# Softmax exponentials per head straight from PSUM on ScalarE, and one vector operation less per weight block, in a pooled-attention and gated-product kernel

## The chip, the cores and the metric

One core of one Trainium2 chip. The metric is device time in microseconds. The engines are named as in the profile: PE is TensorE (its matmuls; PEld are its weight loads), DVE is VectorE, ACT is ScalarE, POOL is GpSimd, SP issues the DMAs. Work on different engines meets through semaphores; each engine takes its own instructions strictly in the order of the program.

## The reference

```python
# q, k, v: 8 x 8 heads x 576 x 64, fp32; k and v are averaged over groups of 8 positions
k_p = k.reshape(B, H, 72, 8, 64).mean(axis=3)
v_p = v.reshape(B, H, 72, 8, 64).mean(axis=3)
scores = scale * np.matmul(q, k_p.transpose(0, 1, 3, 2))
scores = scores - np.max(scores, axis=-1, keepdims=True)
attn = np.exp(scores)
attn = attn / (np.sum(attn, axis=-1, keepdims=True) + 1e-09)
x = np.matmul(attn, v_p)          # put together to 4608 tokens x 512
# the weights arrive as float64: 512 x 1536, 512 x 1536, 1536 x 512
return ((x @ w_a) * (x @ w_b)) @ w_out
```

## The kernel before

**Products.** The 4608 tokens form 9 tiles of 512, and the inner width 1536 forms 12 blocks of 128, so there are 108 steps, x = 0 to 107. `ffn_in(x)` computes block f of x @ w_a into the PSUM tile `psa` and of x @ w_b into `psb`, `gated` multiplies the two (ACT copies `psa` to `h`, DVE multiplies `psb` into it at L528), and `ffn_out(x - 1)` adds the step before to four accumulators `acc`. For accuracy every fp32 operand is split into a high and a low part (`jha`, `jla` and so on), and three products high·high, low·high, high·low are summed. That makes 36 matmuls of 512 columns in a step.

**Splitting the weights.** `split_weight` does it for each step anew: ACT casts the high part (L236), POOL subtracts to get the low part (L171, through the helper `low_part`). The tiles `jh…`, `jl…` have two buffers each.

**Converting the weights.** `convert_weights` runs only in the first tile. For each of 3 matrices and 12 blocks a DMA brings the float64 words into one area per matrix, and fp32 is put together from the bits: ACT takes the magnitude of the high words (`wmag`, L212) and scales the low words (`wlow`, L213); DVE clamps and scales the magnitude (L214), masks and shifts it (L215), sets the sign bit (L219) and adds the low words (L224). After L219 the area is free and the next block's load is issued. Block f + 1 is converted during step f - 1.

**Attention.** `chunk(i)` handles 128 or 64 query rows of one batch, all heads; there are 40 chunks, four of them (`early`, the first tile) before the first step. The scores of two heads (2 · 72 = 144 columns) come from one block-diagonal key tile `kdiag`. For the first 9 chunks (`SUMMED = 9`) each pair of heads takes three matmuls of 144 columns into PSUM (L390), and DVE takes the maximum (L374) and subtracts it (L375) straight from PSUM. The later 31 chunks take one matmul of 288 columns that holds the high and the low key part side by side (L404) and one of 144 (L407); DVE adds the two halves (L410), then takes maximum and difference over all 8 heads. In both forms ACT then takes the exponential of all 576 columns at once (L424), DVE sums it (L426), adds 1e-9 and inverts (L427, L428), POOL scales (L430), and the probabilities are split, transposed on PE (`ptr`, L475), copied out by ACT (`p`, L476) and multiplied with the values (`po`). The PSUM tiles of scores, transposes and values share a ring of two buffers, tag `att` (the four early chunks use the accumulators' buffers for scores).

**Order.** The order of each engine is that in which the Python code emits instructions. `Chains` holds generators that are resumed by a clock of slots: `yield n` sleeps n slots, `yield PE` waits for a turn to put matmuls between those of a step. A step makes six slots, one for each six of its matmuls.

Of the kernel before, what the change touches and what calls it, by code (L numbers as in the profile page):

```python
# [9 lines left out]
F32 = mybir.dt.float32  # L10
F32R = mybir.dt.float32r
I32 = mybir.dt.int32
U32 = mybir.dt.uint32
AF = mybir.ActivationFunctionType
ALU = mybir.AluOpType
AX = mybir.AxisListType

B, H, S, D = 8, 8, 576, 64
POOL = 8
SP = S // POOL  # L20
P = 128
# [4 lines left out]
NF = DF // P  # L26
NK = DM // P

TINY = 2.0**-15
SCALE = 1.0 / float(D) ** 0.5  # L30


# [19 lines left out]
BLOCK, BLOCK_LATER = 256, 384  # L52

NTMP = 6

SUMMED = 9

AHEAD = 2

# [12 lines left out]
class Chains:  # L72
# [4 lines left out]
    PE = "PE"  # L77
# [4 lines left out]
    def mark(self, *what):  # L82
        self.done.add(what)

    def wait(self, *marks):
        while not all(m in self.done for m in marks if not isinstance(m[-1], int) or m[-1] >= 0):
            yield 1
# [26 lines left out]
def attn_moe_kernel(ctx: ExitStack, tc: tile.TileContext, q, k, v, vr, wa, wb, wo, out):  # L114
    nc = tc.nc
    const = ctx.enter_context(tc.tile_pool(name="const", bufs=1))
    sb = ctx.enter_context(tc.tile_pool(name="sb", bufs=2))
    ps = ctx.enter_context(tc.tile_pool(name="ps", bufs=1, space=bass.MemoryType.PSUM))
    chains = Chains()
    PE = Chains.PE  # L120
    mark, wait, done = chains.mark, chains.wait, chains.done
    PRODUCTS, SPLITS, CHUNKS, WEIGHTS, KEYS = ((x, 0) for x in range(5))

    def tmp(name, dtype=F32):
        return sb.tile([P, 512], dtype, tag="tmp", name=name, bufs=NTMP)
# [20 lines left out]
    blocks, start = [], 0  # L146
# [14 lines left out]
    while start < len(flat):  # L161
        stop = start
# [3 lines left out]
        start = stop  # L166
# [28 lines left out]
    def convert_weights(name, j, first):  # L195

        def load_words(f):
            nc.sync.dma_start(area[name], w_dram[name][:, f, :].bitcast(I32))

        load_words(0)
        yield first
        for f in range(NF):
            words = area[name].rearrange("p (c w) -> p c w", w=2)
            hi, lo = words[:, :, 1], words[:, :, 0]
            w = raw[name][:, f, :]
            wi = w.bitcast(I32)  # L210
            low, mag = tmp(f"wlow_{name}{f}", I32), tmp(f"wmag_{name}{f}")
            nc.scalar.activation(mag, hi.bitcast(F32), AF.Abs)  # L212
            nc.scalar.activation(low, lo.bitcast(U32), AF.Copy, scale=2.0**-29)  # L213
            nc.vector.tensor_scalar(out=w, in0=mag, scalar1=TINY, scalar2=2.0**-16, op0=ALU.max, op1=ALU.mult)  # L214
            nc.vector.tensor_scalar(  # L215
                out=wi, in0=wi, scalar1=0x0FFFFFFF, scalar2=3, op0=ALU.bitwise_and, op1=ALU.logical_shift_left
            )
            yield 1
            nc.vector.scalar_tensor_tensor(  # L219
                out=wi, in0=hi, scalar=-(1 << 31), in1=wi, op0=ALU.bitwise_and, op1=ALU.bitwise_or  # L220
            )
            if f + 1 < NF:
                load_words(f + 1)
            nc.vector.tensor_tensor(out=wi, in0=wi, in1=low, op=ALU.add)  # L224
            mark("weight", name, f)
            yield 2

            while f + 1 >= AHEAD and (len(begun) <= f + 1 - AHEAD or chains.now < begun[f + 1 - AHEAD] + 2 * j):
                yield 1
# [116 lines left out]
    def chunk(i):  # L346
        b, o, n = flat[i]
        t, col = divmod(b * S + o, NT)
        first = i < early
# [7 lines left out]
        qh = sb.tile([P, NK, P], F32R, tag="qh", name=f"qh_{i}")  # L357
        ql = sb.tile([P, NK, P], F32R, tag="ql", name=f"ql_{i}")
# [7 lines left out]
        kd = kdiag[b % 2]  # L366
        s = sb.tile([P, H, SP], F32, tag="s", name=f"s_{i}")
        m = sb.tile([P, H], F32, tag="m", name=f"m_{i}")
        z = sb.tile([P, H], F32, tag="z", name=f"z_{i}")
        hk = 2 * SP  # L370

        def less_max(hs, src):
            nh = hs.stop - hs.start
            nc.vector.tensor_reduce(out=m[:n, hs], in_=src, axis=AX.X, op=ALU.max)  # L374
            nc.vector.tensor_tensor(  # L375
                out=s[:n, hs], in0=src, in1=m[:n, hs].unsqueeze(2).broadcast_to([n, nh, SP]), op=ALU.subtract
            )

        if i < SUMMED:
            for g0 in range(0, NK, 2):  # L380
                yield from wait(("keys", b, g0))
                yield PE
                if first:
                    pt = ps.tile([P, 512], F32, tag="acc", name=f"psc_{i}_{g0}", bufs=4)
                else:
                    pt = ps.tile([P, 512], F32, tag="att", name=f"psc_{i}_{g0}", bufs=2)
                for j in range(2):
                    g = g0 + j
                    for x, (qq, w) in enumerate(((qh, 0), (qh, 1), (ql, 0))):
                        nc.tensor.matmul(  # L390
                            pt[:n, j * hk:(j + 1) * hk],
                            qq[:, g, :n],
                            kd[:, g, w].rearrange("p e s -> p (e s)"),
                            start=(x == 0),
                            stop=(x == 2),
                        )
                less_max(slice(2 * g0, 2 * g0 + 4), pt[:n, :2 * hk].rearrange("p (h s) -> p h s", h=4))
        else:
            for g in range(NK):
                yield from wait(("keys", b, g - g % 2))  # L400
                if g % 2 == 0:
                    yield PE
                pt = ps.tile([P, 512], F32, tag="att", name=f"psc_{i}_{g}", bufs=2)
                nc.tensor.matmul(  # L404
                    pt[:n, :2 * hk], qh[:, g, :n], kd[:, g].rearrange("p w e s -> p (w e s)"), start=True, stop=False
                )
                nc.tensor.matmul(  # L407
                    pt[:n, :hk], ql[:, g, :n], kd[:, g, 0].rearrange("p e s -> p (e s)"), start=False, stop=True
                )
                nc.vector.tensor_reduce(  # L410
                    out=s[:n, 2 * g:2 * g + 2, :].rearrange("p h s -> p (h s)"),
                    in_=pt[:n, :2 * hk].rearrange("p (w c) -> p c w", w=2),
                    axis=AX.X,
                    op=ALU.add,
                )
                if g % 2 and g < NK - 1:
                    yield 1
            yield 1
            less_max(slice(0, H), s[:n])
        mark("scores", i)  # L420


        yield 1
        nc.scalar.activation(s[:n], s[:n], AF.Exp, scale=SCALE)  # L424
        yield 1
        nc.vector.tensor_reduce(out=z[:n], in_=s[:n], axis=AX.X, op=ALU.add)  # L426
        nc.vector.tensor_scalar_add(z[:n], z[:n], 1e-9)  # L427
        nc.vector.reciprocal(z[:n], z[:n])  # L428
        yield 1
# [1 line left out]
            out=s[:n], in0=s[:n], in1=z[:n].unsqueeze(2).broadcast_to([n, H, SP]), op=ALU.mult  # L431
# [17 lines left out]
        j = block_of[i]  # L449
# [47 lines left out]
        for g0 in range(0, NK, per):  # L497
# [6 lines left out]
            for g in range(g0, g0 + per):  # L504
                if per == NK and g == NK // 2:
# [9 lines left out]
                    start=False,  # L515
                    stop=True,
# [41 lines left out]
    acc = {}  # L558
# [27 lines left out]
    with tc.manual_schedule():  # L586
        load_early()
        nc.vector.tensor_copy(ident, ident0)
        for t in kdiag + vdiag:
            nc.gpsimd.memset(t.bitcast(F32), 0.0)  # L590
        nc.vector.tensor_reduce(
            out=mask[:NR], in_=ident0[:NR, :NR].rearrange("p (a c s) -> p c a s", a=3, c=4), axis=AX.XY, op=ALU.add
        )
        chains.start(load_keys(0), KEYS)
        for i in range(early):
            chains.start(chunk(i), (CHUNKS[0], i), EARLY_GAP * i)
# [3 lines left out]
        for j, name in enumerate(("a", "b", "o")):  # L600
            chains.start(convert_weights(name, j, CONVERT_AFTER + 2 * j), WEIGHTS, WEIGHTS_START)
# [6 lines left out]
        for i in range(early, len(flat)):  # L608
            b, o, n = flat[i]
            end = TILE_SLOTS * (b * S + o + n) // NT - TILE_SLOTS  # L610
            if tile_of[i] == 1:
                end = TILE_SLOTS - (tail[-1] - i) * CHUNK_GAP
            begin_at = max(0, end - (CHUNK if tile_of[i] == 1 else CHUNK_LATER))
            chains.start(chunk(i), (CHUNKS[0], i), begin_at)
            if i + 1 < len(flat) and flat[i + 1][0] > max(b, 1):
                keys_at = max(0, begin_at - KEYS_AHEAD)
                chains.start(load_keys(b + 1), KEYS, keys_at)
                chains.start(load_values(b + 1), KEYS, keys_at + VALUES_AFTER)
# [65 lines left out]
```

## Time and profile before

| | |
|---|---|
| median of 3 runs | 1110.5 us (1110.24 to 1191.36) |
| profiled execution | 1109.42 us, its span 1107.6 us |
| granted TensorE clock, mean over the span | 0.972 |
| PE busy | 1036.8 us (94%), 4964 matmuls |
| DVE busy | 601.3 us (54%) |
| ACT busy | 523.2 us (47%) |
| POOL busy | 565.4 us (51%) |
| HBM | 49.28 MB read, 9.44 MB written |

The profiled execution and the span differ by 1.8 us that lie around the first and the last instruction. A row of a group reads: line, engine, operation, tiles written and read, shapes, count; busy us and mean ns of one; idle time of the engine just before them, and what ended it. A row of the timeline reads: start, duration, engine, line, operation, tiles, shapes, count, and in brackets the idle time before it.

### The profile page before, as it was taken

How to read it: one execution, taken by the hardware profiler on the slowest of the kernel's cores; microseconds unless marked ns; L12 is line 12 of the kernel's file. 1: busy time of each engine (PE TensorE's matmuls, PEld its weight loads, DVE VectorE, ACT ScalarE, POOL GpSimd, SP SyncE). 2: the span in 40 equal slices, each digit the busy share in tenths (PEclk: the TensorE clock that was granted, in tenths of full speed). 3: DMA queues.
4: the chain of work that ended last, by engine and by line, in shares of the span. 5: the costliest groups of instructions: out<-in, count | busy, mean ns of one | idle time of the engine just before them, and what ended most of it. 6: DMA issues, size and time to landing. Idle time of an engine off the chain costs nothing.

```text
span 1107.6 us, 13659 instructions
## 1 busy us (share of the span) xinstructions
PE 1036.8 (94%) x4964; PEld 861.5 (78%) x4964; DVE 601.3 (54%) x953; ACT 523.2 (47%) x1051; POOL 565.4 (51%) x465
## 2 busy tenths in 40 slices
PE   4378887899999999999999999999999999999998
PEld 4256765688887888888888888888888888888887
DVE  8889899963348333753367335653458343332111
ACT  3654555544445445544455445444445444443332
POOL 6234353455555555555555455554556455554442
PEclk9778888999999999999999999999999999999999
DMA  6444343220023000400021002200211020001001
GB/s 221 124 142 124 121 129 120 74 89 1 1 70 111 1 1 22 148 3 1 1 94 59 1 1 91 81 1 1 69 55 48 1 67 1 1 1 38 1 1 38
DMA packets 29875, 59.59 MB, mean 54 GB/s; under 512 B 7121, under 2 KB 7121, under 8 KB 29809
## 3 DMA queue, kind: packets, MB, share of 16 engines
q1 hardware_dynamic: 29808, 58.73, 16.7%
q8 instruction: 39, 0.64, 0.2%
q14 instruction: 28, 0.22, 0.1%
HBM read 49.28 MB, written 9.44 MB: 53 GB/s over the span
## 4 chain that ended last, share of the span: by engine, by line
PE 82%; DVE 13%; ACT 2%; DMA 1%; issue 1%; POOL 0%; SPq 0%; DVEq 0%; ACTq 0%
PE acc L571 9%; PE psa L550 8%; PE psb L550 8%; PE acc L573 8%; PE acc L572 8%; PE psa L552 8%; PE psa L551 8%; PE psb L551 8%; PE psb L552 8%; PE ptr L475 2%; PE psc L404 2%; DVE wb_raw L224 1%; DVE wa_raw L224 1%; DVE wo_raw L224 1%; DVE wb_raw L219 1%
## 5 line engine op out<-in xcount | busy, mean ns | idle before, releaser
L171 POOL TENSOR_TENSOR jlb<-wb_raw,jhb 128x512 fp32r<-128x512 f32 x108 | 142.8, 1322 | 244.6 <-ACT jhb L236 244.6
L528 DVE TENSOR_TENSOR h<-psb,h 128x512 f32<-128x512 f32 x108 | 74.5, 690 | 344.1 <-PE psb L552 334.3
L171 POOL TENSOR_TENSOR jla<-wa_raw,jha 128x512 fp32r<-128x512 f32 x108 | 143.1, 1325 | 196.4 <-ACT jha L236 170.1
L555 ACT COPY h<-psa 128x512 f32<-128x512 f32 x108 | 63.3, 587 | 241.9 <-PE psa L552 234.3
L550 PE MATMUL psb<-xh,jhb 128*128 128x512 f32 x432 | 172.9, 400 | 4.6 <-DVE h L528 4.6
L571 PE MATMUL acc<-jho,hh 128*128 128x512 f32 x432 | 175.7, 407 | 0.0
L550 PE MATMUL psa<-xh,jha 128*128 128x512 f32 x432 | 172.7, 400 | 0.0
L573 PE MATMUL acc<-jho,hl 128*128 128x512 f32 x432 | 170.2, 394 | 0.6 <-DVE hl L171 0.6
L572 PE MATMUL acc<-jlo,hh 128*128 128x512 f32 x432 | 170.0, 393 | 0.0
L552 PE MATMUL psb<-xh,jlb 128*128 128x512 f32 x432 | 170.0, 393 | 0.0
L551 PE MATMUL psb<-xl,jhb 128*128 128x512 f32 x432 | 169.9, 393 | 0.0
L552 PE MATMUL psa<-xh,jla 128*128 128x512 f32 x432 | 169.6, 392 | 0.0
L551 PE MATMUL psa<-xl,jha 128*128 128x512 f32 x432 | 169.3, 392 | 0.0
L171 POOL TENSOR_TENSOR jlo<-wo_raw,jho 128x512 fp32r<-128x512 f32 x108 | 154.3, 1428 | 5.6 <-ACT jho L236 5.6
L531 ACT CAST hh<-h 128x512 fp32r<-128x512 f32 x108 | 67.1, 621 | 84.7 <-DVE h L528 84.6
L171 DVE TENSOR_TENSOR hl<-h,hh 128x512 fp32r<-128x512 f32 x108 | 93.9, 869 | 20.7 <-ACT hh L531 20.5
L550 PEld LDWEIGHTS psb<-xh,jhb 128*128 128x128 f32 x432 | 82.2, 190 | 20.9 <-issue 4.3
L573 PEld LDWEIGHTS acc<-jho,hl 128*128 128x128 f32 x432 | 81.9, 190 | 18.9 <-DVE hl L171 1.0
L552 PEld LDWEIGHTS psb<-xh,jlb 128*128 128x128 f32 x432 | 82.2, 190 | 17.6
L552 PEld LDWEIGHTS psa<-xh,jla 128*128 128x128 f32 x432 | 81.7, 189 | 17.6
L551 PEld LDWEIGHTS psb<-xl,jhb 128*128 128x128 f32 x432 | 82.2, 190 | 15.2
L551 PEld LDWEIGHTS psa<-xl,jha 128*128 128x128 f32 x432 | 82.0, 190 | 15.2 <-DVE xl L171 0.2
(92 smaller groups left out, 1714.4 us busy)
## 6 DMA issues: line engine op xcount, KB each, us to landing
out<-y SPq DMA_DIRECT2D x36, 256.0 KB, 2.2
kraw<-in_k SPq DMA_DIRECT2D x28, 288.0 KB, 3.6
vraw<-in_v SPq DMA_DIRECT2D x28, 256.0 KB, 3.0
qraw<-in_q SPq DMA_DIRECT2D x28, 256.0 KB, 3.7
words<-in_wa SPq DMA_DIRECT2D x12, 512.0 KB, 3.5
words<-in_wb SPq DMA_DIRECT2D x12, 512.0 KB, 3.6
words<-in_wo SPq DMA_DIRECT2D x12, 512.0 KB, 3.5
vraw<-in_vr SPq DMA_DIRECT2D x14, 192.0 KB, 2.5
```

Of the source, the lines that this page charges most:

```text
L171: eng.tensor_tensor(out=lo, in0=src, in1=hi.bitcast(F32), op=ALU.subtract)
L224: nc.vector.tensor_tensor(out=wi, in0=wi, in1=low, op=ALU.add)
L404: nc.tensor.matmul(pt[:n, :2 * hk], qh[:, g, :n], kd[:, g].rearrange("p w e s -> p (w e s)"), start=True, stop=False)
L528: nc.vector.tensor_tensor(out=h, in0=pt, in1=h, op=ALU.mult)
L531: nc.scalar.copy(hh, h)
L550: nc.tensor.matmul(pt, wh[:, c], xh[:, kk], start=(kk == 0), stop=False)
L551: nc.tensor.matmul(pt, wh[:, c], xl[:, kk], start=False, stop=False)
L552: nc.tensor.matmul(pt, wl[:, c], xh[:, kk], start=False, stop=(kk == NK - 1))
L555: nc.scalar.copy(h, pt)
L571: nc.tensor.matmul(acc[c], hh[:, cs], wh, start=(f == 0), stop=False)
L572: nc.tensor.matmul(acc[c], hh[:, cs], wl, start=False, stop=False)
L573: nc.tensor.matmul(acc[c], hl[:, cs], wh, start=False, stop=(f == NF - 1))
```

## The change

Three edits.

1. In `convert_weights` the magnitude comes from ACT already scaled (by 2^-112), the vector operation at L214 goes, and the masking reads ACT's result directly. The count of ACT's instructions stays.
2. In `chunk`, all 40 chunks take the form with three matmuls of 144 columns; the form with 288 columns and its sum goes.
3. The softmax is done per group of four heads: DVE takes the maximum from PSUM and multiplies it by -scale (4 columns), and ACT then runs four exponentials, one for each head, of 72 columns each, from PSUM, with the maximum as bias and with their sums written to `z`. The subtraction, the exponential over 576 columns and the sum on DVE go. All of it is emitted in the slot of the matmuls; one `yield 1` is left before the inversion.

```diff
-            nc.scalar.activation(mag, hi.bitcast(F32), AF.Abs)
+            nc.scalar.activation(mag, hi.bitcast(F32), AF.Abs, scale=SHRINK)
             nc.scalar.activation(low, lo.bitcast(U32), AF.Copy, scale=2.0**-29)
-            nc.vector.tensor_scalar(out=w, in0=mag, scalar1=TINY, scalar2=2.0**-16, op0=ALU.max, op1=ALU.mult)
             nc.vector.tensor_scalar(
-                out=wi, in0=wi, scalar1=0x0FFFFFFF, scalar2=3, op0=ALU.bitwise_and, op1=ALU.logical_shift_left
+                out=wi, in0=mag.bitcast(I32), scalar1=0x0FFFFFFF, scalar2=3, op0=ALU.bitwise_and, op1=ALU.logical_shift_left
             )
...
-        def less_max(hs, src):
-            nh = hs.stop - hs.start
-            nc.vector.tensor_reduce(out=m[:n, hs], in_=src, axis=AX.X, op=ALU.max)
-            nc.vector.tensor_tensor(
-                out=s[:n, hs], in0=src, in1=m[:n, hs].unsqueeze(2).broadcast_to([n, nh, SP]), op=ALU.subtract
-            )
-
-        if i < SUMMED:
...
-        else:
-            for g in range(NK):
...
-                nc.tensor.matmul(
-                    pt[:n, :2 * hk], qh[:, g, :n], kd[:, g].rearrange("p w e s -> p (w e s)"), start=True, stop=False
...
-                nc.tensor.matmul(
-                    pt[:n, :hk], ql[:, g, :n], kd[:, g, 0].rearrange("p e s -> p (e s)"), start=False, stop=True
...
-            less_max(slice(0, H), s[:n])
...
+        for g0 in range(0, NK, 2):
...
+            for j in range(2):
+                g = g0 + j
+                for x, (qq, w) in enumerate(((qh, 0), (qh, 1), (ql, 0))):
+                    nc.tensor.matmul(
...
+            hs = slice(2 * g0, 2 * g0 + 4)
+            scores = pt[:n, :2 * hk].rearrange("p (h s) -> p h s", h=4)
+            nc.vector.tensor_reduce(out=m[:n, hs], in_=scores, axis=AX.X, op=ALU.max)
+            nc.vector.tensor_scalar_mul(m[:n, hs], m[:n, hs], -SCALE)
+            for j in range(4):
+                h = 2 * g0 + j
+                nc.scalar.activation(
+                    s[:n, h], scores[:, j], AF.Exp, bias=m[:n, h:h + 1], scale=SCALE, accum_out=z[:n, h:h + 1]
+                )
         mark("scores", i)
...
-        nc.scalar.activation(s[:n], s[:n], AF.Exp, scale=SCALE)
-        yield 1
-        nc.vector.tensor_reduce(out=z[:n], in_=s[:n], axis=AX.X, op=ALU.add)
         nc.vector.tensor_scalar_add(z[:n], z[:n], 1e-9)
         nc.vector.reciprocal(z[:n], z[:n])
```

ACT's order around chunk 4, the first chunk after the first step, before the change. The numbers behind names count tiles as they are made, and differ between the two programs; `s_632` here and `s_645` below are the same chunk's exponentials, `h_616` and `h_630` the product of step 1.

```order
L212 ACTIVATE wmag_b_621<-words 128x512
L213 ACTIVATE wlow_b_620<-words 128x512
L236 CAST jhb_658<-wb_raw 128x512
L236 CAST jho_661<-wo_raw 128x512
L212 ACTIVATE wmag_o_665<-words 128x512
L213 ACTIVATE wlow_o_664<-words 128x512
L531 CAST hh_655<-h_616 128x512
L424 ACTIVATE s_632<-s_632 64x576
L212 ACTIVATE wmag_a_708<-words 128x512
```

The same place now:

```order
L210 ACTIVATE wmag_b_635<-words 128x512
L211 ACTIVATE wlow_b_634<-words 128x512
L392 ACTIVATE s_645,z_647<-psc_0_653,m_646 64x72 x4
L233 CAST jhb_675<-wb_raw 128x512
L233 CAST jho_678<-wo_raw 128x512
L210 ACTIVATE wmag_o_682<-words 128x512
L211 ACTIVATE wlow_o_681<-words 128x512
L392 ACTIVATE s_645,z_647<-psc_2_686,m_646 64x72 x4
L503 CAST hh_672<-h_630 128x512
```

The exponentials now stand in two groups of four, the first one ahead of the casts and magnitudes that stood ahead of the single exponential before.

DVE's order at the same place, before:

```order
L374 TENSOR_REDUCE m_633<-psc_0_640 64x4
L375 TENSOR_TENSOR s_632<-psc_0_640,m_633 64x288
L528 TENSOR_TENSOR h_616<-psb_1_618,h_616 128x512
L214 TENSOR_SCALAR wo_raw<-wmag_o_665 128x512
L215 TENSOR_SCALAR wo_raw<-wo_raw 128x512
L374 TENSOR_REDUCE m_633<-psc_2_670 64x4
L375 TENSOR_TENSOR s_632<-psc_2_670,m_633 64x288
L219 SCALAR_TENSOR_TENSOR wo_raw<-words,wo_raw 128x512
L224 ISA wo_raw<-wo_raw,wlow_o_664 128x1024
L171 TENSOR_TENSOR hl_656<-h_616,hh_655 128x512
L426 TENSOR_REDUCE z_634<-s_632 64x8
L427 TENSOR_SCALAR z_634<-z_634 64x8
```

And now:

```order
L388 TENSOR_REDUCE m_646<-psc_0_653 64x4
L389 TENSOR_SCALAR m_646<-m_646 64x4
L500 TENSOR_TENSOR h_630<-psb_1_632,h_630 128x512
L212 TENSOR_SCALAR wo_raw<-wmag_o_682 128x512
L388 TENSOR_REDUCE m_646<-psc_2_686 64x4
L389 TENSOR_SCALAR m_646<-m_646 64x4
L399 TENSOR_SCALAR z_647<-z_647 64x8
L400 RECIPROCAL z_647<-z_647 64x8
L216 SCALAR_TENSOR_TENSOR wo_raw<-words,wo_raw 128x512
L221 ISA wo_raw<-wo_raw,wlow_o_681 128x1024
L170 TENSOR_TENSOR hl_673<-h_630,hh_672 128x512
```

The addition to `z`, which needs all eight exponentials, now stands right behind the second maximum; before there were three long operations between the second subtraction and the sum.

PE's order at the first half of a later chunk's scores, before:

```order
L404 MATMUL psc_0_4415<-kdiag_73,qh_4360 128x288
L407 MATMUL psc_0_4415<-kdiag_73,ql_4361 128x144
L404 MATMUL psc_1_4419<-kdiag_73,qh_4360 128x288
L407 MATMUL psc_1_4419<-kdiag_73,ql_4361 128x144
L550 MATMUL psa_5_4400<-xh_3242,jha_4324 128x512
```

And now:

```order
L379 MATMUL psc_0_4499<-kdiag_73,qh_4466 128x144 x2
L379 MATMUL psc_0_4499<-kdiag_73,ql_4467 128x144
L379 MATMUL psc_0_4499<-kdiag_73,qh_4466 128x144 x2
L379 MATMUL psc_0_4499<-kdiag_73,ql_4467 128x144
L522 MATMUL psa_5_4485<-xh_3262,jha_4408 128x512
```

Four matmuls with 864 columns in all became six with the same 864 columns.

More of the change, by code (lines that the diff above doesn't have):

```diff
@@ L27 @@
 NK = DM // P
-TINY = 2.0**-15
+SHRINK = 2.0**-112
 SCALE = 1.0 / float(D) ** 0.5
@@ L54 @@
 NTMP = 6
-SUMMED = 9
 AHEAD = 2
@@ L370, in chunk @@
         hk = 2 * SP
-        def less_max(hs, src):
-            nh = hs.stop - hs.start
-            nc.vector.tensor_reduce(out=m[:n, hs], in_=src, axis=AX.X, op=ALU.max)
-            nc.vector.tensor_tensor(
-                out=s[:n, hs], in0=src, in1=m[:n, hs].unsqueeze(2).broadcast_to([n, nh, SP]), op=ALU.subtract
-            )
-        if i < SUMMED:
[L380 to L384, printed above, removed]
-                else:
[L386 to L398, printed above, removed]
-            for g in range(NK):
[L400 to L404, printed above, removed]
-                    pt[:n, :2 * hk], qh[:, g, :n], kd[:, g].rearrange("p w e s -> p (w e s)"), start=True, stop=False
-                )
-                nc.tensor.matmul(
-                    pt[:n, :hk], ql[:, g, :n], kd[:, g, 0].rearrange("p e s -> p (e s)"), start=False, stop=True
[L409 to L416, printed above, removed]
-                    yield 1
-            yield 1
-            less_max(slice(0, H), s[:n])
@@ new lines, in chunk @@
+        for g0 in range(0, NK, 2):
+            yield from wait(("keys", b, g0))
+            yield PE
+            if first:
+                pt = ps.tile([P, 512], F32, tag="acc", name=f"psc_{i}_{g0}", bufs=4)
+            else:
+                pt = ps.tile([P, 512], F32, tag="att", name=f"psc_{i}_{g0}", bufs=2)
+            for j in range(2):
+                g = g0 + j
+                for x, (qq, w) in enumerate(((qh, 0), (qh, 1), (ql, 0))):
+                    nc.tensor.matmul(
+                        pt[:n, j * hk:(j + 1) * hk],
+                        qq[:, g, :n],
+                        kd[:, g, w].rearrange("p e s -> p (e s)"),
+                        start=(x == 0),
+                        stop=(x == 2),
+                    )
[7 more added lines that the diff above has]
+                    s[:n, h], scores[:, j], AF.Exp, bias=m[:n, h:h + 1], scale=SCALE, accum_out=z[:n, h:h + 1]
+                )
@@ L420, in chunk @@
         mark("scores", i)
         yield 1
-        nc.scalar.activation(s[:n], s[:n], AF.Exp, scale=SCALE)
-        yield 1
-        nc.vector.tensor_reduce(out=z[:n], in_=s[:n], axis=AX.X, op=ALU.add)
         nc.vector.tensor_scalar_add(z[:n], z[:n], 1e-9)
```

## The prediction

> **What bounds the kernel now.** I read the chain that ended last, then busy time by stretch, then the groups of instructions in the stretch where the stage changes.
>
> ```profile
> PE 82%; DVE 13%; ACT 2%; DMA 1%; issue 1%; POOL 0%; SPq 0%; DVEq 0%; ACTq 0%
> 0.00:60.00 60.00, 25.59 (x122) 23.19 (x123) 50.17 (x87) 28.71 (x62) 25.50 (x35) 0.86 0.55 178
> 60.00:207.00 147.00, 116.03 (x512) 92.78 (x511) 134.99 (x199) 81.34 (x162) 61.85 (x46) 0.85 0.39 120
> 207.00:250.00 43.00, 41.40 (x209) 34.42 (x208) 29.84 (x44) 20.82 (x41) 23.33 (x18) 1.00 0.24 79
> 250.00:1108.00 858.00, 853.80 (x4127) 711.13 (x4125) 386.34 (x626) 392.34 (x788) 454.68 (x368) 1.00 0.10 33
> ```
>
> The columns of the last four rows are length, then busy us of PE, PEld, DVE, ACT, POOL, then granted clock, DMA share, GB/s. Two regimes meet at about 207 us. From 250 on PE is busy 853.8 of 858 us at clock 1.00, and nothing but fewer or shorter matmuls helps. From 60 to 207, while ten blocks of each weight matrix are converted, DVE is busy 134.99 of 147 us (92%) and PE's clock drops to 0.85 in its gaps. The 13% of DVE in the chain lie here and in the 60 us before. So each part of the change is priced by regime: on DVE before 207, on PE after.
>
> **Part 1: the vector operation at L214 goes.** These are its groups in the 60:207 stretch, with the spread of one of them over the whole run, and two neighbours that met no other engine.
>
> ```profile
> L214 DVE TENSOR_SCALAR wb_raw<-wmag_b 128x512 f32<-128x512 f32 x10 | 6.0, 596 | 2.0 <-ACT wmag_b L212 2.0
> L214 DVE TENSOR_SCALAR wa_raw<-wmag_a 128x512 f32<-128x512 f32 x10 | 5.4, 536 | 1.5 <-ACT wmag_a L212 1.5
> L214 DVE TENSOR_SCALAR wo_raw<-wmag_o 128x512 f32<-128x512 f32 x10 | 5.1, 515 | 1.4 <-ACT wmag_o L212 1.4
> L214 DVE TENSOR_SCALAR wa_raw<-wmag_a x12: 367/420/1516, 34.9 to 194.6; 128x512 f32<-128x512 f32 x12
> 78.88 0.42 DVE L214 TENSOR_SCALAR wb_raw<-wmag_b 128x512 f32<-128x512 f32 x1
> 79.33 0.43 DVE L215 TENSOR_SCALAR wb_raw<-wb_raw 128x512 int32<-128x512 int32 x1
> ```
>
> Thirty of them cost 16.5 us as recorded, but the median is 420 ns and some reach 1516. From one start to the next it is 0.45 us (79.33 - 78.88), so 30 x 0.45 = 13.5 us; the other 3 us are stretches in which an instruction was held up. I count 13.5: a hold that L214 no longer takes falls on L215 behind it. The Trainium skill, "SBUF — State Buffer", section "Who interferes with whom", says why that is likely: a DVE operation in a two-port mode and a GpSimd operation lock each other out for a whole instruction. By that rule the removal gains 13.5 us, without it 16.5.
>
> Ahead of the first step, six more L214 stand in the chain that ends last; these four are its pieces of them, and the wait that follows.
>
> ```profile
> 34.94 0.35 DVE wa_raw L214
> 42.47 0.44 DVE wa_raw L214
> 45.94 1.29 DVE wo_raw L214
> 49.01 0.35 DVE wb_raw L214
> 50.47 3.53 DMA words<-in_wo
> ```
>
> They add up to 2.4 us, of which some 0.9 in the third are a hold (1.29 against 0.42). I take 2 us: the load of `words` for `wo` is issued that much earlier, and ACT's queue (`wmag_o`, then the copies of `ptr`, then the first step) with it. The casts, DMAs and SP's queue keep their order. Sum of part 1: -15.5 us, and nothing after 207, where no conversion runs.
>
> **Part 2: three matmuls of 144 columns in place of 288 and 144.** The first six rows are half a later chunk as it is now, up to the second matmul after it; the last six are half of chunk 8, which has the new form already.
>
> ```profile
> 410.76 0.29 PE L404 MATMUL psc<-kdiag,qh 128*128 128x288 f32 x1
> 410.89 0.23 PE L407 MATMUL psc<-kdiag,ql 128*128 128x144 f32 x1
> 410.95 0.34 PE L404 MATMUL psc<-kdiag,qh 128*128 128x288 f32 x1
> 411.13 0.23 PE L407 MATMUL psc<-kdiag,ql 128*128 128x144 f32 x1
> 411.20 0.44 PE L550 MATMUL psa<-xh,jha 128*128 128x512 f32 x1
> 411.48 0.39 PE L551 MATMUL psa<-xl,jha 128*128 128x512 f32 x1
> ...
> 183.33 0.34 PE L390 MATMUL psc<-kdiag,qh 128*128 128x144 f32 x2
> 183.51 0.28 PE L390 MATMUL psc<-kdiag,ql 128*128 128x144 f32 x1
> 183.62 0.39 PE L390 MATMUL psc<-kdiag,qh 128*128 128x144 f32 x2
> 183.84 0.27 PE L390 MATMUL psc<-kdiag,ql 128*128 128x144 f32 x1
> 183.96 0.43 PE L550 MATMUL psb<-xh,jhb 128*128 128x512 f32 x1
> 184.23 0.39 PE L551 MATMUL psb<-xl,jhb 128*128 128x512 f32 x1
> ```
>
> Half a chunk moves from 411.48 - 410.76 = 0.72 us to 184.23 - 183.33 = 0.90: the columns are equal, but six weight loads stand in place of four, and short matmuls do not cover them. That is 0.36 us for a chunk. Of the 31 chunks, 25 have 128 rows: +9.0 us. The six with 64 rows load half as many columns of weights; they cost between 0 and 0.36 us each, and I take 0. PE has no slack there, so all of it counts: **+9.0 us**, at most 11.2. This is the surest term.
>
> **Part 3: the softmax per group.** From 250 on I count it at nothing. DVE loses work, ACT gains some, and the cover is that weight parts are ready long before use:
>
> ```profile
> 401.26 1.29 POOL L171 TENSOR_TENSOR jla<-wa_raw,jha 128x512 fp32r<-128x512 f32 x1 [2.50 <-ACT jha L236]
> 409.85 0.39 PE L552 MATMUL psa<-xh,jla 128*128 128x512 f32 x1
> ```
>
> `jla`, done at 402.55, is first read at 409.85, 7.3 us later; a group of exponentials that holds ACT for 2 us is hidden. In the `att` ring the next tile after a chunk's second scores comes six slots later, so four slow readers hold nobody up.
>
> Before 207 it is otherwise. Chunks 4 to 8 fall there. What DVE saves, per chunk, and what it adds:
>
> ```profile
> L426 DVE TENSOR_REDUCE z<-s 128x8 f32<-128x576 f32 x3 | 2.2, 745 | 0.0
> L375 DVE TENSOR_TENSOR s<-psc,m 128x288 f32<-128x288 f32 x6 | 2.7, 458 | 0.4
> L427 DVE TENSOR_SCALAR z<-z 128x8 f32<-128x8 f32 x3 | 1.2, 401 | 0.1
> ```
>
> Two L375 and one L426 go: 2 x 0.46 + 0.74 = 1.66 us. Two operations on 4 columns come; the nearest is L427, 0.40 us in this stretch: 0.80. So DVE's work falls by 0.86 us, 4.3 in five chunks. But now ACT stands between DVE's own instructions, and its rows price the wait.
>
> ```profile
> 78.95 0.60 ACT L236 CAST jhb<-wb_raw 128x512 fp32r<-128x512 f32 x1
> 79.46 0.61 ACT L236 CAST jho<-wo_raw 128x512 fp32r<-128x512 f32 x1
> 79.98 0.68 ACT L212 ACTIVATE wmag_o<-words 128x512 f32<-128x512 f32 x1
> 86.34 0.68 ACT L424 ACTIVATE s<-s 64x576 f32<-64x576 f32 x1 [1.01 <-DVE s L375]
> 91.28 0.39 ACT L441 CAST rem<-s 64x64 fp32r<-64x64 f32 x2
> 28.38 0.65 ACT L267 ACTIVATE kdiag<-kp 64x144 fp32r<-64x144 f32 x2
> ```
>
> No row has an exponential of 72 columns with a bias and a sum. Two casts of 64 columns take 0.39 us together, two scalings of 144 columns 0.65; above, one instruction cannot cost more than the whole of 576 columns, 0.68. Four are thus 0.7 to 2.7 us, and I take 1.1, near the scalings. By the Trainium skill, "ScalarE: Activation LUTs", section "What ACT_TABLE_LOAD costs", a per-partition bias adds about 93 ns to an activation; an estimate from its figures is 1.1 us for four as well, without the sum; no row here has such a bias.
>
> The wait comes twice in a chunk. After the first maximum DVE soon needs a `wmag` that now stands behind the exponentials and what follows them on ACT. In chunks 4 and 7 that is 1.1 + 0.51 + 0.52 + 0.68 = 2.8 us, less 0.6 for `h` on DVE: 2.2. In chunks 5 and 8 only the copy of `h` (about 0.5) stands between: 2.3. In chunk 6 nothing does, and `hl` covers 0.6: 1.2. After the second maximum `z` needs the second group: 1.1 us and a hop, 1.2. Sum: 2 x 2.2 + 2 x 2.3 + 1.2 + 5 x 1.2 = 16.2 us. Against it stand the waits for `wmag` that DVE has now, 2.0 + 1.5 + 1.4 = 4.9 us in L214's rows; about 3.4 come after an exponential and go. That leaves +12.8 us. While DVE waits, POOL finishes operations that would have held it later; with POOL busy 61.85 of 147 us, that gives back between 0 and 0.42 x 12.8 = 5.4, and I take 2. Net of part 3: -4.3 + 12.8 - 2 = **+6.5 us**. In chunks 0 to 3 DVE saves about as much as ACT adds; I count 0, within 3 us either way.
>
> **Sum.** -15.5 + 9.0 + 6.5 = 0 on the profiled execution's own 1109.42 us, of which 1107.6 are its span; the median of the runs shown, 1110.5, is 0.1% above. Forecast: **1109 us**, no change that a measurement of this kernel tells from none, which takes about 2% (22 us).
>
> **The rivals.**
>
> *The waits hide.* If ACT's groups mostly fall into DVE's stalls, part 3 is -4.3 in place of +6.5: 1098 us; with L214's holds gone too (another 3), 1095. For it: DVE is idle 12 of 147 us already, and PE runs ahead of it, so scores are ready early. Against it: `z` stands directly behind the second maximum, and nothing is between to fill that hole.
>
> *Exponentials cost what the wide one does.* If summing makes each of the eight cost 0.68 us, each group takes 2.7 in place of 1.1, and five chunks wait twice 1.6 us longer: +16, 1125 us. It turns slower than before at the 0.275 us for one exponential that I took, since the sum is 0 there; each further tenth of a microsecond adds 4 us, and over 2% it would need 0.84. For it: fixed cost dominates small rows (240 ns for 64 columns). Against it: 144 columns take 0.33.
>
> *The conversion does not hang on DVE.* If the loads of `words` or ACT's order set the pace there, L214's removal moves nothing, and part 1 is 0: 1109 + 15.5 = 1125. For it: DMAs of 3.5 us stand in the early chain. Against it: 92% DVE busy and ACT busy 81 of 147.
>
> **How the numbers follow.** Forecast, 1103 to 1115: 0.57. Waits hidden, 1091 to 1103: 0.23. Dear exponentials, 1115 to 1130: 0.12. Conversion not on DVE, 1115 to 1128: 0.08. The range that leaves out 2 in 10 is 1095 to 1120: the low end has waits hidden and holds gone, the high end 0.5 us for one exponential (+9) and all of PE's upper bound (+2.2). Faster by over 2% (below 1088) needs more than the first rival gives: 0.06. Slower by over 2% (above 1132) needs both others together: 0.05. Between: 0.89.
>
> **What would show it.** In the profile after: 124 more matmuls; scores of 128 rows at about 0.90 us for each half chunk up to the second matmul behind; no holes on PE from 250 on; L212 (the old L215) with a larger mean hold and new waits for `wmag`; `z`'s addition waiting for ACT about 1.2 us in chunks 4 to 8; ACT's exponentials near 0.27 us from start to start; the first step starting at about 57.7 in place of 59.66; the conversions done at about 198 in place of 207. The prediction is wrong if the first 250 us shrink by over 15 us, if an exponential's start-to-start is over 0.4, or if PE waits for weight parts late in the run.

## The result, and the profile after

The changed kernel takes **1127.0 us** (median of 4 runs), the kernel before 1110.5 us beside it: a ratio of 1.0149, with a 95% interval of 1.0129 to 1.0169. That is 16.5 us slower. One of the four runs of the kernel before, at 1191.36 us, fell in a slower state of the chip and is left out of these figures. The forecast was 1109 us, and the time lies above its range, 1095 to 1120. The prediction took 2% as what a measurement of this kernel needs; the interval is 0.2% to either side, so the loss is clear. The profiled span went from 1107.6 to 1124.8 us.

First the shares of the chain that ended last, where PE had 82% and ACT 2% before:

```profile
PE 76%; DVE 13%; ACT 6%; issue 3%; DMA 1%; SPq 0%; DVEq 0%; ACTq 0%
```

Then the stages, in the columns of the prediction's table (length, busy us of PE, PEld, DVE, ACT, POOL, granted clock, DMA share, GB/s):

```profile
0.00:60.00 60.00, 24.94 (x119) 22.80 (x120) 41.94 (x77) 35.81 (x121) 26.93 (x35) 1.00 0.54 178
60.00:207.00 147.00, 118.10 (x541) 93.42 (x541) 121.21 (x171) 94.60 (x245) 65.76 (x48) 0.91 0.40 124
207.00:250.00 43.00, 42.25 (x216) 35.60 (x214) 24.20 (x35) 22.77 (x69) 22.84 (x18) 1.00 0.20 67
250.00:1125.00 875.00, 862.72 (x4218) 720.41 (x4217) 362.26 (x534) 441.61 (x1217) 458.37 (x365) 0.99 0.10 32
```

DVE did get lighter, by 13.8 us in 60:207, and ACT heavier by 13.3. The stage that was full is no longer full: from 250 on PE was idle for 4.2 of 858 us before, and now for 12.3 of 875.

A second view locates that. Take the start of each of the 108 steps (its first `psa` matmul) in both traces. The changed kernel is 5.5 us ahead at step 13 (227 us). Behind that it loses 0.37 us for each chunk of 128 rows, evenly, and has **three jumps**, each over three or four steps: 4.4 us at 340 to 376 us, 2.7 at 598 to 640, 2.9 at 858 to 891. Some 3 us more go in smaller steps, which were not traced one by one. At the first jump, PE waits for a copy of `ptr` (the third transpose takes the buffer of the `att` ring that this copy frees), and ACT's copy stands behind `hh`, which waits for DVE. These rows are PE, ACT, then DVE and POOL in order of time:

```profile
353.26 0.28 PE L447 MATMUL ptr<-ident,rem 64*96 64x64 f32 x2 [3.52 <-ACT p L448]
352.23 0.62 ACT L503 CAST hh<-h 128x512 fp32r<-128x512 f32 x1 [4.18 <-DVE h L500]
344.06 6.81 DVE L328 SCALAR_TENSOR_TENSOR vdiag<-vp,vdiag 64x256 fp32r<-64x256 f32 x2
350.79 0.68 DVE L170 TENSOR_TENSOR vrem<-vwide,vrem 32x512 fp32r<-32x512 f32 x1
351.50 0.69 DVE L500 TENSOR_TENSOR h<-psb,h 128x512 f32<-128x512 f32 x1
343.65 1.49 POOL L402 TENSOR_TENSOR s<-s,z 64x576 f32<-64x576 f32 x1 [4.40 <-DVE z L400]
345.11 1.29 POOL L170 TENSOR_TENSOR jla<-wa_raw,jha 128x512 fp32r<-128x512 f32 x1
346.49 1.36 POOL L170 TENSOR_TENSOR pr<-s,pr 64x512 fp32r<-64x512 f32 x1
347.80 0.33 POOL L170 TENSOR_TENSOR rem<-s,rem 64x64 fp32r<-64x64 f32 x1
348.08 1.28 POOL L170 TENSOR_TENSOR jlb<-wb_raw,jhb 128x512 fp32r<-128x512 f32 x1
349.33 1.25 POOL L170 TENSOR_TENSOR jlo<-wo_raw,jho 128x512 fp32r<-128x512 f32 x1
```

Two operations on `vdiag` (the low part of a new batch's values) take 6.81 us on DVE, as long as POOL's row of six operations lasts without a pause. In the kernel before the same two took 1.91 us, and POOL's scaling of `s` came only eight microseconds later:

```profile
345.44 1.91 DVE L331 SCALAR_TENSOR_TENSOR vdiag<-vp,vdiag 64x256 fp32r<-64x256 f32 x2
353.56 1.33 POOL L430 TENSOR_TENSOR s<-s,z 64x576 f32<-64x576 f32 x1
```

The schedule counts in slots (the `yield` numbers). The old softmax had three more of them between a later chunk's scores and POOL's scaling: one between the two halves of the scores, one ahead of the maximum over all heads, one behind the exponential. With them gone, POOL's row of the chunk moved on top of DVE's work for the next batch's values. That was the theory to be tried; its rival was that eight exponentials at a time hold ACT, whatever the slots.

### The profile page after: what moved, and what is told of

The parts are those of the page before. It is cut to its first block, busy times and chain, and to the rows that moved or that the text cites. A ratio compares the mean times of both kernels' runs of the same rounds, so it can differ in the third digit from the quotient of the medians.

```text
span 1124.8 us, 14426 instructions
## 1 busy us (share of the span) xinstructions
PE 1048.0 (93%) x5088; PEld 872.2 (78%) x5088; DVE 549.6 (49%) x815; ACT 594.8 (53%) x1651; POOL 573.9 (51%) x465
## 4 chain that ended last, share of the span: by engine, by line
PE 76%; DVE 13%; ACT 6%; issue 3%; DMA 1%; SPq 0%; DVEq 0%; ACTq 0%
PE psb L522 8%; PE psa L522 8%; PE psa L524 8%; PE psa L523 8%; PE psb L524 7%; PE psb L523 7%; PE acc L543 7%; PE acc L544 7%; PE acc L545 7%; PE psc L379 3%; ACT s L392 3%; DVE vdiag L328 2%; PE ptr L447 2%; DVE h L500 1%; DVE hl L170 1%
## 5 line engine op out<-in xcount | busy, mean ns | idle before, releaser
L170 POOL TENSOR_TENSOR jla<-wa_raw,jha 128x512 fp32r<-128x512 f32 x108 | 155.4, 1439 | 93.0 <-ACT jha L233 88.1
L522 PE MATMUL psb<-xh,jhb 128*128 128x512 f32 x432 | 178.4, 413 | 3.1 <-DVE h L500 3.1
L543 PE MATMUL acc<-jho,hh 128*128 128x512 f32 x432 | 171.2, 396 | 0.0
L392 ACT ACTIVATE s<-psc,m 128x72 f32<-128x72 f32 (+1 forms) x320 | 97.9, 318 | 133.8 <-DVE m L389 133.2
L170 DVE TENSOR_TENSOR hl<-h,hh 128x512 fp32r<-128x512 f32 x108 | 130.3, 1206 | 38.2 <-ACT hh L503 38.0
L402 POOL TENSOR_TENSOR s<-s,z 128x576 f32<-128x576 f32 (+1 forms) x38 | 46.3, 1218 | 198.9 <-PE psb L524 122.1
```

Source lines behind the costliest of these rows:

```text
L170: eng.tensor_tensor(out=lo, in0=src, in1=hi.bitcast(F32), op=ALU.subtract)
L392: nc.scalar.activation(s[:n, h], scores[:, j], AF.Exp, bias=m[:n, h:h + 1], scale=SCALE, accum_out=z[:n, h:h + 1])
L402: (nc.vector if first and i % 2 else nc.gpsimd).tensor_tensor(out=s[:n], in0=s[:n], in1=z[:n].unsqueeze(2).broadcast_to([n, H, SP]), op=AL ...
L522: nc.tensor.matmul(pt, wh[:, c], xh[:, kk], start=(kk == 0), stop=False)
L543: nc.tensor.matmul(acc[c], hh[:, cs], wh, start=(f == 0), stop=False)
```

## The experiments

All times are medians; each ratio is to runs of the kernel before on the same chip. Where an expectation speaks of the three later batches, the edit reaches all seven batches after the first; the jumps are at three of them.

### One part at a time

The weights' edit alone, on the kernel before:

```diff
-nc.scalar.activation(mag, hi.bitcast(F32), AF.Abs)
+nc.scalar.activation(mag, hi.bitcast(F32), AF.Abs, scale=SHRINK)
-nc.vector.tensor_scalar(out=w, in0=mag, scalar1=TINY, scalar2=2.0**-16, ...)
-nc.vector.tensor_scalar(out=wi, in0=wi, ...)
+nc.vector.tensor_scalar(out=wi, in0=mag.bitcast(I32), ...)
```

> The kernel before with the weights' edit alone (the magnitude scaled in its activation, 36 vector operations fewer). Theory: DVE sets the pace to 207 us, and part 1 is worth the 15.5 us of the prediction: about 1095 us, the first step at about 57.7 us in place of 59.7, and no change in what stands after 250 us. Rival: the conversion does not hang on DVE (the loads of words or ACT's queue set it): 1109 to 1111 us.

Measured: 1097.0 us, 0.9876 (0.9862 to 0.9891), **-13.2 us**. The rival falls: the conversion does hang on DVE. Step 13 starts 12.6 us earlier, and PE has no hole from 250 on:

```profile
250.00:1095.00 845.00, 841.11 (x4065) 700.71 (x4063) 382.96 (x619) 386.02 (x774) 446.31 (x360) 1.00 0.10 33
```

But the first step starts at 59.75 us, as before, and not at 57.7. The chain of waits says why:

```profile
49.24 4.61 DMA words<-in_wo
53.94 0.66 ACT wmag_o L213
```

The load of `words` for `wo` is issued 1.2 us earlier than before (49.24 against 50.47) and takes 1.1 us longer (4.61 against 3.53). It lands at the same time. Why it took longer is not shown.

The columns alone, with the old softmax operations:

```diff
-SUMMED = 9
+SUMMED = 40
```

> The kernel before with the three matmuls of 144 columns in all chunks (they were in chunks 0 to 8 only) and the softmax in its old operations, two slots earlier from chunk 9 on since that form has fewer of them. Theory: 0.37 us for each chunk of 128 rows, about +9 us, 1120 us, with no jump at 344, 601 and 861 us. Rival 1: the jumps come from the slots that go missing, not from the exponentials: two of the four slots are gone here, so jumps of 1 to 4 us stand at those three places as well, 1123 to 1130. Rival 2: the columns cost nothing and the +0.37 us for each chunk is the exponentials' doing: 1111 us.

Measured: 1119.4 us, 1.0079 (1.0064 to 1.0094), **+9.2 us**, with 0.37 us for each chunk of 128 rows. Two of the three missing slots are missing here too, and the largest PE gap from 250 us on is 0.5 us. So those two slots alone make no jump.

Everything but the weights' edit:

```diff
-nc.scalar.activation(mag, hi.bitcast(F32), AF.Abs, scale=SHRINK)
+nc.scalar.activation(mag, hi.bitcast(F32), AF.Abs)
+nc.vector.tensor_scalar(out=w, in0=mag, scalar1=TINY, scalar2=2.0**-16, ...)
-nc.vector.tensor_scalar(out=wi, in0=mag.bitcast(I32), ...)
+nc.vector.tensor_scalar(out=wi, in0=wi, ...)
```

> The changed kernel with the weights' conversion as it was before (36 vector operations on DVE more). Theory: the weights' edit still gains its 15.5 us inside the changed kernel, so this one takes about 1142 us, with the three jumps at their places. Rival: with the exponentials on ACT the conversion waits for ACT anyway, and the edit gains at most the 5 us that are seen at step 13: 1127 to 1132 us.

Measured: 1141.2 us, 1.0277 (1.0261 to 1.0292), +31.1 us, with the three jumps. The weights' edit is worth 14 to 15 us inside the changed kernel. With the columns' 9.2 taken off, the softmax part alone costs about 22 us. The forecast had 6.5.

### Where the softmax part's 22 us are

The changed kernel with three slots put back:

```diff
+            if i >= 9 and g0 < NK - 2:
+                yield 1
         mark("scores", i)
         yield 1
+        if i >= 9:
+            yield 1
+            yield 1
```

> The changed kernel with three slots put back into the chunks from 9 on (one between the two halves of the scores, two ahead of the addition on z), so that the scaling of s on POOL stands in the schedule about where it stood before. Theory: the three jumps come from POOL's chain of a chunk (the scaling, then the low parts of pr and rem, with jla, jlb between) standing beside DVE's two operations on vdiag at L328: they vanish, the late run shows no PE gap over 1 us, and the time falls by about 10 us to 1117. Rival: four exponentials at a time on ACT hold the copies wherever they stand: 1125 to 1128 us.

Measured: 1116.1 us, 1.0046 (1.0030 to 1.0063): 11 us less than the changed kernel, with the same exponentials. The rival falls. Four small holes of 0.8 to 1.1 us remain at the same places, so "vanish" was a little too much.

The changed kernel with nothing moved but the two operations on `vdiag` (and `vrem` behind them):

```diff
         nc.scalar.copy(vrf[:NR], wide[:NR])
+        if b:
+            yield 4
```

> The changed kernel with nothing altered but that the two vector operations on vdiag (L328), for the three later batches, come four slots later. Theory: the three jumps are DVE's L328 pair held by POOL's row of operations of the chunk (6.8, 4.3 and 4.3 us there); moved out of that row they take about 0.45 us each, the copies of ptr are not late, and the time falls by 8 to 11 us to 1116 to 1119. Rival 1: the exponentials on ACT hold the copies: 1125 to 1128 us. Rival 2: any DVE operation with two operands in SBUF that stands there is held, so the next one (hl or ql) is late in place of L328 and at most half of the gain comes: 1121 to 1124 us.

Measured: **1113.2 us**, 1.0022 (1.0012 to 1.0031), better than the theory's range: PE's busy time from 250 to 1090 us rises from 831.8 to 839.0 of 840. The pair now starts in a pause of POOL; the operation that stands in its old place is held instead, 2.74 us, as rival 2 had it, but nothing urgent follows it:

```profile
346.82 2.74 DVE L170 TENSOR_TENSOR ql<-qraw,qh 128x256 fp32r<-128x256 f32 x1 [1.30 <-ACT qh L358]
349.48 1.84 DVE L330 SCALAR_TENSOR_TENSOR vdiag<-vp,vdiag 64x256 fp32r<-64x256 f32 x2
```

The counter-test takes the slots out of the kernel before, which has one exponential for all heads:

```diff
-                if g % 2 and g < NK - 1:
-                    yield 1
-            yield 1
             less_max(slice(0, H), s[:n])
 ...
         nc.scalar.activation(s[:n], s[:n], AF.Exp, scale=SCALE)
-        yield 1
+        if first or i < SUMMED:
+            yield 1
```

> The kernel before, with its own softmax and its own columns, but three slots taken out of the chunks from 9 on, so that the scaling of s on POOL stands in the schedule where the changed kernel has it. Theory: the jumps are a matter of slots and not of exponentials per head: stalls of PE of 1.5 to 4 us stand at about 344, 601 and 861 us here too, and the time is 5 to 10 us above the kernel before: 1115 to 1120 us. Rival: they need ACT's eight exponentials as well: 1109 to 1111 us.

Measured: 1143.4 us, 1.0294 (1.0277 to 1.0311), **+32 us** with no edit of an operation. The same pair, the same chain (DVE, then ACT, then PE):

```profile
354.63 5.54 DVE L331 SCALAR_TENSOR_TENSOR vdiag<-vp,vdiag 64x256 fp32r<-64x256 f32 x2
362.59 0.62 ACT L529 CAST hh<-h 128x512 fp32r<-128x512 f32 x1 [4.58 <-DVE h L526]
363.62 0.36 PE L473 MATMUL ptr<-ident,rem 64*96 64x64 f32 x2 [4.68 <-ACT p L474]
```

The direction is the theory's, and the exponentials are not needed for it. The size is not: 5 to 10 us were expected. The three holes are longer than in the changed kernel (4.7, 3.6 and 3.6 us against 3.5, 1.5 and 1.5), and there are more of them, of 2.0 us at 231, 491 and 752 us. Not all of the 32 us is traced.

Next, the pair stays in its place and POOL computes it, so that DVE has nothing there to be held:

```diff
+            if b:
+                nc.gpsimd.tensor_tensor(out=vp[r, :NK], in0=vp[r, :NK], in1=share[r]..., op=ALU.mult)
+                low_part(nc.gpsimd, vd[r, :, 1, r], vp[r, :NK], vd[r, :, 0, r])
+                continue
             nc.vector.scalar_tensor_tensor(out=vd[r, :, 1, r], ...)
```

> The changed kernel with the low part of vdiag for the later batches at its own place in the schedule, but computed by POOL in two steps for each half (a multiplication, then the subtraction) in place of one operation on DVE each. Theory: DVE was held by POOL, so with nothing for POOL to hold, h at L500 comes in time, no PE gap over 1 us stands at 344 to 355, 600 to 610 and 860 to 870 us, and the time is 1113 to 1118 us, though POOL's row there grows by 2 to 3 us. Rival 1: the copies of p are late because of POOL's own row (the scaling of s, then pr and rem): with a longer row the gaps grow and the time is 1127 to 1135 us. Rival 2: ACT's exponentials hold the copies: 1127 us.

Measured: 1128.9 us, 1.0165 (1.0147 to 1.0183). The first half of the theory holds: `h` starts 2.6 us behind POOL's scaling of `s` (349.84 - 347.20), where it was 7.9 in the changed kernel (351.50 - 343.65). The time is that of the first rival: POOL's row grew, and PE waits for `pr` instead. (The second rival, ACT's exponentials, names about the same time, but the wait is on POOL.)

```profile
347.20 1.49 POOL L410 TENSOR_TENSOR s<-s,z 64x576 f32<-64x576 f32 x1 [4.40 <-DVE z L408]
349.84 0.69 DVE L508 TENSOR_TENSOR h<-psb,h 128x512 f32<-128x512 f32 x1
349.34 1.07 POOL L172 TENSOR_TENSOR vdiag<-vp,vdiag 64x256 fp32r<-64x256 f32 x1
353.31 1.70 POOL L172 TENSOR_TENSOR pr<-s,pr 64x512 fp32r<-64x512 f32 x1
355.06 0.50 PE L455 MATMUL ptr<-ident,pr 64*128 64x64 f32 x4 [2.26 <-POOL pr L172]
```

So DVE's hold is what made `h` late, and it can be taken away; but this way only trades it for a wait on POOL, whose row has no room for the work either.

### What the exponentials cost before 250 us

Without the sums (`z` from the first column of each head):

```diff
-    s[:n, h], scores[:, j], AF.Exp, bias=..., scale=SCALE, accum_out=z[:n, h:h + 1]
+    s[:n, h], scores[:, j], AF.Exp, bias=..., scale=SCALE
-nc.vector.tensor_scalar_add(z[:n], z[:n], 1e-9)
+nc.vector.tensor_scalar_add(z[:n], s[:n, :, 0], 1e-9)
```

> The changed kernel without the sums: the exponentials do not accumulate, and z is made from the first column of each head in place of the sum, so it still waits for the exponentials. Theory: the second instruction that each accumulating exponential brings (205 ns, on ACT's own queue) is part of the 0.295 us from start to start; without it four take 0.2 us each or a little more, the waits before 207 us shorten by 0.3 to 0.4 us each, about -4 us: 1123. Rival: 0.295 us is the exponential's own time and the second instruction is hidden in it: 1127 us, with the same start-to-start.

Measured: 1117.6 us, 1.0063 (1.0048 to 1.0078), 9 us less. These rows are ACT of the changed kernel at chunk 4, and then the same place without sums:

```profile
85.99 0.32 ACT L392 ACTIVATE s<-psc,m 64x72 f32<-64x72 f32 x1 [1.28 <-DVE m L389]
86.21 0.19 ACT L392 ACTIVATION_READ_ACCUMULATOR s<-psc,m 64x1 f32 x1
86.30 0.30 ACT L392 ACTIVATE s<-psc,m 64x72 f32<-64x72 f32 x1
87.19 0.62 ACT L503 CAST hh<-h 128x512 fp32r<-128x512 f32 x1
```

```profile
83.73 0.93 ACT L392 ACTIVATE s<-psc,m 64x72 f32<-64x72 f32 x4 [1.26 <-DVE m L389]
84.55 0.62 ACT L503 CAST hh<-h 128x512 fp32r<-128x512 f32 x1
```

Each exponential with a sum is two instructions, and four hold ACT for 1.20 us (87.19 - 85.99); without sums for 0.82. The theory's mechanism holds, its size does not: 4.3 of the 9 us are there at step 13; part of the rest is PE gaps that are each 0.4 us shorter, and the remainder isn't traced.

One slot more ahead of the addition on `z` in chunks 0 to 8, beside the old slots (the edit is against the run with old slots):

```diff
         yield 1
+        yield 1
         if i >= 9:
-            yield 1
             yield 1
```

> The changed kernel with the old slots from chunk 9 on, as in the run with old slots (1116.1 us), and one slot more ahead of the addition on z in chunks 0 to 8 as well. Theory: in chunks 0 to 8 the vector queue stands still at the addition on z until the second four exponentials are done, some 1.2 us a chunk in chunks 4 to 8; a slot later they are done already, and the time falls by 4 to 6 us to 1111. Rival: the wait moves to the next operation on DVE that needs ACT (the conversion's), or the later probabilities make PE wait: 1115 to 1118 us.

Measured: 1113.8 us, 1.0026 (1.0015 to 1.0037), 2.3 us less than with the old slots alone: between the two. The waits on DVE (engine, line, releaser, total us, times, longest) between 60 and 207 us, of the changed kernel and then of this one:

```profile
DVE z L399 <- ACT s L392: 7.5, 5, 1.5
DVE wb_raw L212 <- ACT wmag_b L210: 4.9, 2, 2.5
DVE wo_raw L212 <- ACT wmag_o L210: 4.9, 2, 2.4
DVE wa_raw L212 <- ACT wmag_a L210: 1.9, 2, 1.4
```

```profile
DVE wo_raw L212 <- ACT wmag_o L210: 10.3, 5, 2.4
DVE wb_raw L212 <- ACT wmag_b L210: 5.8, 4, 2.5
DVE wa_raw L212 <- ACT wmag_a L210: 4.0, 3, 1.4
```

The 7.5 us at `z` go, and the waits for the conversion's magnitudes rise from 11.7 to 20.1 us: ACT is late for DVE either way.

### Two combinations

The changed kernel with both the later `vdiag` and the extra slot in the early chunks:

> The changed kernel with the operations on vdiag four slots later (1113.2 us alone) and one slot more ahead of the addition on z in chunks 0 to 8 (worth 2.3 us beside the old slots). Theory: the two lie in different stages and add up: 1111 us. Rival: the gain of the slot was chance in the order of DVE's early work: 1113 us or more.

Measured: 1109.9 us, 0.9995 (0.9985 to 1.0004). The two add up (3.3 us below the run with later values), and the whole change is then worth nothing either way.

The weights' edit on the kernel before, with the later `vdiag`:

> The kernel before with the weights' edit (1097.0 us alone) and the two operations on vdiag four slots later for the later batches. Theory: with the old slots that pair was held for 1.9 us in all and no PE gap followed, so the later place gains nothing: 1096 to 1097 us. Rival: the late run of the kernel before hides small losses at these places too: 1094 to 1095 us.

Measured: 1109.0 us, 0.9985 (0.9973 to 0.9997): 12 us *worse* than the weights' edit alone, which neither theory had. With the old slots the later place is the bad one. The pair now takes 1.80 us, and `hl` behind it is held by POOL's `pr`, `rem` and `jla`; the scores' sum is late, and PE waits:

```profile
342.30 3.32 DVE L172 TENSOR_TENSOR hl<-h,hh 128x512 fp32r<-128x512 f32 x1
346.87 0.50 PE L406 MATMUL psc<-kdiag,qh 128*64 128x288 f32 x1 [2.89 <-DVE s L412]
```

So "later" is no cure by itself. What counts is whether a DVE operation that POOL can hold starts beside POOL's row with urgent work behind it. The version that beats both kernels is the weights' edit alone, 1097.0 us.

## Why the prediction was wrong, point by point

The terms, each beside its measurement:

| term | forecast | measured | from |
| --- | --- | --- | --- |
| part 1, the weights | -15.5 | -13.2 | weights alone |
| part 2, the columns | +9.0 | +9.2 | columns alone |
| part 3, before 250 us | +6.5 | +6.2 | run with later values: +2.2 + 13.2 - 9.2 |
| part 3, from 250 on | 0 | +14.3 | changed kernel (+16.5) less that run (+2.2) |
| sum | 0 | +16.5 | |

The split of part 3 takes the run with later values as free of the late loss. The starts of the steps give a second reading of the late term: behind step 13 the changed kernel loses 22.7 us and the run with the columns alone 9.6, which leaves 13.1.

- **The step that failed is "From 250 on I count it at nothing."** The term that stood at nothing measured 13 to 14 us. I named ACT's slack (weight parts 7.3 us ahead) and the `att` ring as the cover. For what I had asked of them both held: from 250 us on PE waits for no weight part, and no reader of scores holds the ring up. But the wait came in that same ring, at the copies of `ptr` (total us, times, longest):

```profile
PE ptr L447 <- ACT p L448: 7.7, 5, 3.5
```

  I did not follow what the missing slots do to POOL: its scaling of `s` and the low parts of `pr` and `rem` moved beside DVE's work on the next batch's values. That it would be wrong "if PE waits for weight parts late in the run" named the wrong tile: PE waited for copies of `ptr`, and these for `hh` and `h`.
- **Part 1** was right in mechanism. Missing are the 2 us of the early chain: I let an earlier issue count as an earlier landing. Without the early term the prediction had 13.5 us by the rule of the Trainium skill, "SBUF — State Buffer", section "Who interferes with whom", and 16.5 us without that rule. The 13.2 us measured are near the first, though one number does not show the rule.
- **Part 2** is right to 0.2 us. Half a later chunk takes 412.88 - 411.98 = 0.90 us:

```profile
411.98 0.34 PE L379 MATMUL psc<-kdiag,qh 128*128 128x144 f32 x2
412.16 0.27 PE L379 MATMUL psc<-kdiag,ql 128*128 128x144 f32 x1
412.27 0.39 PE L379 MATMUL psc<-kdiag,qh 128*128 128x144 f32 x2
412.49 0.28 PE L379 MATMUL psc<-kdiag,ql 128*128 128x144 f32 x1
412.60 0.44 PE L522 MATMUL psa<-xh,jha 128*128 128x512 f32 x1
412.88 0.39 PE L523 MATMUL psa<-xl,jha 128*128 128x512 f32 x1
```

- **Part 3 before 207** came out near its size. By another reading, step 13 starts 5.8 to 6.6 us later with later values or old slots than with the weights' edit alone, some 0.6 us of which are the columns (step 13 starts 0.56 us later with the columns alone). Waits for `wmag` rose by 6.8 us (4.9 + 4.9 + 1.9 against 4.9), as the forecast's 10.2 less 3.4 has it; the waits at `z` are 7.5 us, forecast 6.0. Together that is 1.5 us more waiting than forecast. What DVE saves (4.3) and what POOL gives back (2) were not measured apart, so that the net came out so near is in part luck. Four exponentials hold ACT 1.20 us, forecast 1.1: right, though without knowing of the second instruction. The conversions end at 202 us, forecast 198, before 207.
- **The rivals.** Dear exponentials (1125) and a conversion not on DVE (1125) come near the time, and both mechanisms are false: an exponential takes 0.30 us from start to start and not 0.68, and 13.2 us were gained on DVE. The case that happened was not on the list.

## What to carry to other kernels

A change that takes steps out of a scheduled chain moves everything behind them on every engine; "it is all hidden" has to be shown for each queue that then stands beside another, not only for the engine whose work changed. When DVE and POOL share a stage, compare their rows at the places where extra work arrives (here a new batch's values), since an operation held there delays all that stands behind it in order. And price the parts of a change apart: here one of three carried all of the gain, and alone it takes 1097 us where the whole takes 1127.

## What the hardware showed

- A DVE operation with two operands in SBUF can be held through several POOL instructions in a row, not one. These are the 16 operations on `vdiag` in the kernel before and in the changed kernel (least, median and longest ns). The row below them is a scaling of four columns, with a single operand, in the run with old slots, beside `pr`, `rem` and `jla` on POOL:

```profile
L331 DVE SCALAR_TENSOR_TENSOR vdiag<-vp,vdiag x16: 404/422/1485, 21.0 to 846.8; 64x256 fp32r<-64x256 f32 x16
L328 DVE SCALAR_TENSOR_TENSOR vdiag<-vp,vdiag x16: 911/1450/4149, 20.6 to 863.4; 64x256 fp32r<-64x256 f32 x16
```

```profile
351.76 2.35 DVE L389 TENSOR_SCALAR m<-m 64x4 f32<-64x4 f32 x1
```

  The Trainium skill, "SBUF — State Buffer", section "Who interferes with whom", has it that a DVE instruction with two SBUF inputs contends with a GpSimd instruction that reads SBUF, and that one with at most one SBUF input, outside the 2-port modes, does not. The trace agrees on both: `h`, which reads one operand from PSUM, took 0.69 us beside POOL's 1.07 us operation in the run with the values on POOL. How long a hold can last is read from the rows: 4.15 us for one operation, beside a row of POOL without a pause whose longest instruction took 1.49. Whether the kind of operand alone decides was not tried.
- An accumulating activation is followed by an instruction of its own that reads the sum: 0.30 us from start to start for 72 columns (1.20 us for four), and 0.21 without (0.82).
- After some of these PE holes the clock falls. Behind the 3.52 us one:

```profile
353.00:359.00 6.00, 5.74 (x27) 0.72 0.00 0
```

The columns are length, PE busy, clock, DMA share, GB/s. Six 512-column matmuls there take 0.42 to 0.52 us to the next start in place of 0.23, about 1.3 us in all. The same followed the holes of 1.54 us that end at 609 and 869 us. It followed only one of the three holes of 2.0 us in the run without slots, and none of those of 0.8 to 1.1 us in the run with old slots. What decides it was not tried.
